# Issuing the first half of the first K load ahead of the wq load in a decode-attention kernel

## Chip, cores and metric

The kernel runs on one core of one Trainium2 chip. The metric is device time in microseconds (us) of one execution; lower is better. Five engines work side by side: TensorE (PE) for matmuls and transposes, VectorE (DVE) and ScalarE (ACT) for element-wise work, GpSimd (POOL), and SyncE (SP), which here only issues transfers. They are carried by 16 DMA engines.

A ratio is formed by the measuring program from the fast runs of both kernels in the same rounds; it is not quite the ratio of the medians quoted beside it, and its 95% interval is 3 to 4 us wide. The experiments ran in three sets of rounds, each on another chip, and each is compared with the kernel before in its own rounds.

## The reference

One token attends over a cache of 65,536 positions in 8 K/V heads of 256 elements, with 16 query heads; a small token-mixer branch and a gate are added. Cut to what matters:

```python
q = (x @ wq).reshape(B, Sq, Hq, Dh).transpose(0, 2, 1, 3)      # x: 1 x 448, wq: 448 x 4096
scores = jnp.einsum("bhqd,bhkd->bhqk", q, k) * (Dh ** -0.5)    # k: 8 heads x 65536 x 256
p = _softmax(scores, axis=-1)
o = jnp.einsum("bhqk,bhkd->bhqd", p, v)                        # v as k
a = o.transpose(...).reshape(B, Sq, Hq * Dh) @ wo
# ... b: layernorm, gelu mixer on the same token; g: sigmoid gate
return g * a + (1 - g) * b
```

K and V are 268 MB each in bf16. Everything else is small: wq is 3.67 MB, wo as much.

## The kernel before

The cache is walked in 32 rounds, each with one K load and one V load of 8.39 MB (64 KB a partition). K goes into a ring of one and a half loads (`kring`), V into one buffer (`vbuf`). SyncE issues every large load, in this order of waits (ScalarE issues the few small ones):

```python
@block.sync
def _(eng):
    eng.dma_start(wq_a..., A_wq[0:WF * P, :]...).then_inc(sem_wq, 16)     # 3.15 MB, into vbuf
    eng.dma_start(wq_b, A_wq[WF * P:DM, :]...).then_inc(sem_wq, 16)       # 0.52 MB, into vbuf
    for j in range(NP):                                                   # NP = 32
        if j >= 1:
            eng.wait_ge(sem_tr[NB - 1], BODY * (j - 1) + DC)   # half of K(j-1) transposed
        if j == 0:
            load(kring, A_k_cache, j, HV, NV, 0, sem_k)        # first half of K0
            load(kring, A_k_cache, j, 0, HV, 0, sem_kb)        # second half of K0
        # ... last round in halves
        else:
            load(kring, A_k_cache, j, 0, NV, HV * (j % 2), sem_k)
        if j == 0:
            eng.wait_ge(s_q, 1)                                # the query is computed: wq is free
            eng.wait_ge(s_hb, 1)
        else:
            eng.wait_ge(sem_pv, j)                             # V(j-1) is used up
        load(vbuf, A_v_cache, j, 0, NFIRST if last else NV, 0, sem_v)
        # ... at the first round of a head: the wo rows of that head
```

V0 overwrites the part of `vbuf` in which wq lies, so it waits for the query. V1 overwrites V0, so it waits until TensorE has done the whole first round: the query, 128 column groups of K0 transposed, scored and turned into weights, then 128 matmuls on V0:

```python
for g in heads:  for m in rounds_of_a_head:        # hardware loops
    keys(c0, j, u16, ...)      # transposes (line 298), scores (318)
    values(j, c0, u16)         # 128 matmuls on vbuf (358), the last one raises sem_pv
```

The softmax here doesn't subtract the row's maximum and nothing guards it: scores larger than these inputs give would overflow.

Of the kernel before, what the change touches and what calls it, by code (L numbers as in the profile page):

```python
# [12 lines left out]
def bass_gated_mix__gqa_block_cached__mixer_token_mlp__decode_kernel(  # L13
# [20 lines left out]
    DM = A_x.shape[-1]  # L34
# [4 lines left out]
    P = 128  # L39
# [17 lines left out]
    WF = 3  # L57
# [34 lines left out]
    with ctx:  # L92
# [6 lines left out]
        def new_sem(name):  # L99
            return ctx.enter_context(nc.semaphore(name))  # L100
# [22 lines left out]
        wq_a = early[:, 0:WF * NQ].rearrange("p (j n) -> p j n", j=WF)  # L123
        wq_b = early[:, WF * NQ:WF * NQ + HALF]
# [57 lines left out]
        sem_wq = new_sem("sem_wq")  # L182
# [36 lines left out]
        def src(cache, j, n0=0, n1=NV):  # L219
            g, m = divmod(j, PPH)  # L220
            s = cache[0, g, m * BODY * CH:(m + 1) * BODY * CH, :].rearrange("(p n) d -> p n d", p=P)
            return s[:, n0:n1, :].rearrange("p n d -> p (n d)")

        @block.sync
        def _(eng):
            eng.dma_start(wq_a.rearrange("p j n -> p (j n)"),  # L226
                          A_wq[0:WF * P, :].rearrange("(p j) n -> p (j n)", p=P)).then_inc(sem_wq, 16)
            eng.dma_start(wq_b, A_wq[WF * P:DM, :].rearrange("r (a n) -> (r a) n", a=2)  # L228
                          ).then_inc(sem_wq, 16)
            def load(dst, cache, j, n0, n1, at, sem):  # L230
                eng.dma_start(dst[:, at + n0:at + n1, :].rearrange("p n d -> p (n d)"), src(cache, j, n0, n1)  # L231
                              ).then_inc(sem, 16)

            for j in range(NP):
                last = j == NP - 1
                if j >= 1:
                    eng.wait_ge(sem_tr[NB - 1], BODY * (j - 1) + DC)
                if j == 0:
                    load(kring, A_k_cache, j, HV, NV, 0, sem_k)
                    load(kring, A_k_cache, j, 0, HV, 0, sem_kb)  # L240
                elif last:
                    load(kring, A_k_cache, j, 0, HV, HV, sem_k)
                    load(kring, A_k_cache, j, HV, NV, HV, sem_kb)
# [3 lines that stand above are left out]
                    eng.wait_ge(s_q, 1)  # L247
                    eng.wait_ge(s_hb, 1)
                else:
                    eng.wait_ge(sem_pv, j)  # L250
                load(vbuf, A_v_cache, j, 0, NFIRST if last else NV, 0, sem_v)
                if last:
                    for (n0, n1), sem in zip(pieces, sem_vp):
                        load(vbuf, A_v_cache, j, n0, n1, 0, sem)
                g, m = divmod(j, PPH)
                if m == 0 and g < H - 1:
                    if g >= 1:
                        eng.wait_ge(s_proj, g)
                    w = A_wo[g * REP * DH:(g + 1) * REP * DH, :]
                    eng.dma_start(wo_rows, w.rearrange("(p i) n -> p (i n)", i=2 * REP)).then_inc(sem_wo, 16)  # L260

            eng.wait_ge(s_proj, H - 1)
            for h in range(REP):
                w = A_wo[(HQ - REP + h) * DH:(HQ - REP + h + 1) * DH, :]
                eng.dma_start(wo_sb[:, h, :], w.rearrange("(p j) n -> p (j n)", j=2)).then_inc(sem_wl[h], 16)  # L265
            eng.wait_ge(s_fin, NCG)
            eng.dma_start(out_ap, out_row[:, :]).then_inc(sem_out, 16)
            eng.wait_ge(sem_out, 16)
# [13 lines left out]
        def _(pe):  # L282
# [86 lines left out]
            def piece_wait(n):  # L369
                for (n0, _), sem in zip(pieces, sem_vp):  # L370
                    if n == n0:
                        pe.wait_ge(sem, 16)
# [335 lines left out]
```

## Time and profile before

| | before |
|---|---|
| median of 6 executions | 1265.95 us (1265.83 to 1266.22) |
| span of the profiled execution | 1264.0 us |
| SyncE's DMA queue under way | 99.7% of 16 engines' span |
| rate from HBM | 431 GB/s |
| TensorE busy | 73% |

The kernel is a stream of loads. Two numbers describe each load: when SyncE issues it, and when it lands (its issue plus the "us to landing" of the DMA view). If each load is issued well ahead of the landing of the one in front of it, the queue never stands. This is the **lead**.

### The profile page before, as it was taken

What the parts mean: (1) busy time and instruction counts of PE and PEld (TensorE: products, weight loads), DVE (VectorE), ACT (ScalarE), POOL (GpSimd) and SP (SyncE); (2) the same over time, 40 slices, a digit from 0 to 9 for tenths busy, and PEclk for the clock granted to TensorE, in tenths of its full rate; (3) what the DMA queues carried; (4) which work ended last, traced back from release to release, by engine and by line L of the source; (5) the groups of instructions that cost most, each with busy time, mean ns of one, the idle gap of its engine ahead of it and who ended that gap; (6) DMA issues with size and microseconds to landing.
All of it is one profiled execution on the core that took longest, in us unless ns stands there. A gap on an engine that the chain in (4) does not pass through costs nothing.

```text
span 1264.0 us, 38850 instructions
## 1 busy us (share of the span) xinstructions
PE 917.0 (73%) x17114; PEld 868.4 (69%) x17114; DVE 422.5 (33%) x764; ACT 538.2 (43%) x788; POOL 0.9 (0%) x7
## 2 busy tenths in 40 slices
PE   3876678766778667786676876758767688676688
PEld 2766668766677666786666876658766578666687
DVE  2433344333444333443222332323322233332233
ACT  1443345533355433454333553335533355433455
POOL 0000000000000000000000000000000000000000
PEclk9887788787898887987888987889887888877999
DMA  9999999999999999999999999999999999999998
GB/s 411 428 434 436 433 431 431 431 438 431 433 433 433 433 431 438 425 433 440 431 436 429 431 431 433 440 433 433 431 431 431 438 436 433 431 433 431 431 427 367
DMA packets 11623, 544.39 MB, mean 431 GB/s; under 512 B 1369, under 2 KB 1628, under 8 KB 2908
## 3 DMA queue, kind: packets, MB, share of 16 engines
q1 hardware_dynamic: 11522, 544.22, 99.7%
q8 instruction: 8, 0.13, 0.0%
q10 hardware_dynamic: 90, 0.01, 0.0%
q14 instruction: 3, 0.02, 0.0%
HBM read 544.22 MB, written 0.00 MB: 431 GB/s over the span
## 4 chain that ended last, share of the span: by engine, by line
DMA 70%; PE 29%; issue 1%; SPq 0%; DVEq 0%; DVE 0%; ACT 0%; ACTq 0%
DMA kring<-in_A_k_cache_dram 68%; PE kst L298 24%; PE sps L318 4%; DMA wo_sb<-in_A_wo_dram 2%; PE acc L358 0%; SPq L231 0%; SPq L265 0%; SPq L228 0%; SPq L226 0%; PE prj L405 0%; PE acc L347 0%; DVEq L92 0%; DVE out_row L634 0%; ACT pT L658 0%; ACTq L658 0%
## 5 line engine op out<-in xcount | busy, mean ns | idle before, releaser
L298 PE MATMUL kst<-ident,kring 128*128 128x128 f32 x4096 | 563.7, 299 | 304.9 <-DMA kring<-in_A_k_cache_dram 294.1
L669 ACT ACTIVATE ktT<-kst 128x1024 bf16<-128x1024 bf16 x512 | 500.0, 1021 | 667.3 <-PE kst L298 666.5
L298 PEld LDWEIGHTS kst<-ident,kring 128*128 128x128 f32 x4096 | 514.0, 156 | 314.8 <-issue 312.2
L569 DVE COPY ktT<-kst 128x1024 bf16<-128x1024 bf16 x512 | 354.2, 692 | 765.0 <-PE kst L298 742.0
L318 PEld LDWEIGHTS sps<-qcur,ktT 128*128 128x128 bf16 x8192 | 237.8, 96 | 4.1 <-issue 1.6
L318 PE MATMUL sps<-qcur,ktT 128*128 128x2 bf16 x8192 | 236.6, 163 | 1.3 <-issue 1.3
L358 PE MATMUL acc<-vbuf,pT 128*2 128x256 bf16 x4080 | 140.4, 305 | 3.8 <-issue 3.3
L358 PEld LDWEIGHTS acc<-vbuf,pT 128*2 128x2 bf16 x4080 | 105.2, 93 | 30.6 <-issue 3.8
L658 ACT ACTIVATE pT<-sps 128x32 f32 x256 | 51.8, 202 | 16.4 <-PE sps L318 16.4
L347 PE MATMUL acc<-pT,ones_sq 128*128 128x32 bf16 x256 | 11.7, 178 | 12.3 <-ACT pT L658 12.3
L347 PEld LDWEIGHTS acc<-pT,ones_sq 128*128 128x128 bf16 x256 | 8.6, 96 | 15.2 <-ACT pT L658 14.9
L675 ACT ACTIVATE z_b<-z_b 128x448 bf16<-128x448 bf16 x14 | 8.1, 577 | 20.5 <-DVE z_b L556 20.4
L575 DVE COPY accs<-acc 128x288 f32<-128x288 f32 x8 | 3.7, 458 | 38.5 <-PE acc L358 38.5
L394 PEld LDWEIGHTS acc<-sel,accs 128*64 128x64 f32 x112 | 10.8, 214 | 0.9
L394 PE MATMUL acc<-sel,accs 128*64 128x1 f32 x112 | 11.4, 260 | 0.0
L431 PE MATMUL acc<-vbuf 42*128 42x42 bf16 x1 | 0.2, 214 | 8.3 <-DMA b_b<-in_B_b_dram 8.3
L405 PE MATMUL prj<-wo_sb,oTn 128*1 128x112 bf16 x128 | 3.7, 244 | 3.1 <-DVE oTn L600 2.9
L431 PEld LDWEIGHTS acc<-vbuf 42*128 42x128 bf16 x1 | 0.1, 102 | 8.4 <-DMA b_b<-in_B_b_dram 8.4
L562 DVE TENSOR_TENSOR gu<-wtmp,z_b 128x448 bf16<-128x448 bf16 x14 | 5.5, 393 | 1.0
L554 DVE TENSOR_TENSOR z_b<-u_b,wtmp 128x448 bf16<-128x448 bf16 x14 | 5.5, 393 | 1.0
L550 DVE TENSOR_TENSOR z_b<-wtmp,u_b 128x448 bf16<-128x448 bf16 x14 | 5.5, 393 | 1.0
L548 DVE TENSOR_TENSOR wtmp<-u_b 128x448 bf16<-128x448 bf16 x14 | 5.5, 392 | 1.1
(89 smaller groups left out, 82.5 us busy)
## 6 DMA issues: line engine op xcount, KB each, us to landing
kring<-in_A_k_cache_dram SPq DMA_DIRECT2D x4, 4096.0 KB, 24.3
vbuf<-in_A_v_cache_dram SPq DMA_DIRECT2D x1, 6144.0 KB, 25.7
wo_sb<-in_A_wo_dram SPq DMA_DIRECT2D x7, 448.0 KB, 27.6
vbuf<-in_A_wq_dram SPq DMA_DIRECT2D x1, 3072.0 KB, 10.2
vbuf<-in_A_v_cache_dram SPq DMA_DIRECT2D x1, 1024.0 KB, 27.8
vbuf<-in_A_v_cache_dram SPq DMA_DIRECT2D x1, 768.0 KB, 28.9
vbuf<-in_A_wq_dram SPq DMA_DIRECT2D x1, 512.0 KB, 10.9
vbuf<-in_A_v_cache_dram SPq DMA_DIRECT2D x31, 29.7
```

The lines of the kernel that those rows point to most:

```text
L298: ins = pe.transpose(kst[:, b, i * P:(i + 1) * P], kring_f[:, at + NT * (k % DC) + 4 * b + i, :], ident[:, :])
L318: ins = pe.matmul(sps[:, par, 2 * nt:2 * nt + 2], ktT[:, par, b, ntl * DH + dj:(ntl + 1) * DH:2], qcur[:, dj, :], start=(dj == 0), stop=(d ...
L347: pe.matmul(acc[:, DENC:SELC], ones_sq[:, :], pT[:, r, :], start=False, stop=(r == BODY - 1), skip_group_check=True)
L358: ins = pe.matmul(acc[o:o + REP, 0:DH], pT[:, r, 2 * nt:2 * nt + 2], vbuf[:, n, :], start=False, stop=False, skip_group_check=True)
L394: ins = pe.matmul(dst[hh * HP:(hh + 1) * HP, i:i + 1], accs[:, i:DH:2 * REP], sel[:, hh:hh + 1], start=False, stop=True, skip_group_check= ...
L548: vec.tensor_tensor(W, U, U, op=ALU.mult)
L550: vec.tensor_tensor(Z, W, U, op=ALU.mult)
L554: vec.tensor_tensor(Z, U, W, op=ALU.add)
L569: vec.tensor_copy(ktT[:, k % KTB, b, :], kst_b[:, b, :]).then_inc(sem_ev[b], 1)
L658: act.activation(pT[:, bass.ds(p0 + k % DC, 1), :].rearrange("p o n -> p (o n)"), sps[:, k % 2, 0:2 * NT], AF.Exp, scale=scale).then_inc(s ...
L669: act.activation(ktT[:, k % KTB, b, :], kst_b[:, b, :], AF.Copy).then_inc(sem_ev[b], 1)
L675: act.activation(z_b[:, :], z_b[:, :], AF.Tanh).then_inc(s_tanh, 1)
```

## The change

Before, PE sits idle for 9.5 us between the end of the query work and the first K transposes. The change lets the first half of K0 come in before wq, so that K should be there when PE gets to it. Nothing is removed or added.

```diff
         def _(eng):
-            eng.dma_start(wq_a.rearrange("p j n -> p (j n)"),
-                          A_wq[0:WF * P, :].rearrange("(p j) n -> p (j n)", p=P)).then_inc(sem_wq, 16)
-            eng.dma_start(wq_b, A_wq[WF * P:DM, :].rearrange("r (a n) -> (r a) n", a=2)
-                          ).then_inc(sem_wq, 16)
 ...
                 if j == 0:
                     load(kring, A_k_cache, j, HV, NV, 0, sem_k)
+                    eng.dma_start(wq_a.rearrange("p j n -> p (j n)"),
+                                  A_wq[0:WF * P, :].rearrange("(p j) n -> p (j n)", p=P)).then_inc(sem_wq, 16)
+                    eng.dma_start(wq_b, A_wq[WF * P:DM, :].rearrange("r (a n) -> (r a) n", a=2)
+                                  ).then_inc(sem_wq, 16)
                     load(kring, A_k_cache, j, 0, HV, 0, sem_kb)
```

## The prediction

> **What bounds the kernel now.** I read the page first: who is busy, and the chain that ended last.
>
> ```profile
> span 1264.0 us, 38850 instructions
> ...
> PE 917.0 (73%) x17114; PEld 868.4 (69%) x17114; DVE 422.5 (33%) x764; ACT 538.2 (43%) x788; POOL 0.9 (0%) x7
> ...
> q1 hardware_dynamic: 11522, 544.22, 99.7%
> ...
> HBM read 544.22 MB, written 0.00 MB: 431 GB/s over the span
> ...
> DMA 70%; PE 29%; issue 1%; SPq 0%; DVEq 0%; DVE 0%; ACT 0%; ACTq 0%
> ```
>
> The queue that SyncE (SP) fills has packets under way for 99.7% of 16 engines' span, while TensorE (PE) has a quarter of the span free. The chain names DMA for 70% and PE for 29%, but a chain that goes from a load's landing back to its issue and from there to the PE work that freed the buffer does not say that the queue was empty while PE worked. So the second view is when each load is issued and when it lands. The lines below are the queue's own timeline for the first 110 us.
>
> ```profile
> 0.74 0.41 SPq L226 DMA_DIRECT2D vbuf<-in_A_wq_dram  x1
> 1.20 0.41 SPq L228 DMA_DIRECT2D vbuf<-in_A_wq_dram  x1
> 1.67 1.10 SPq L231 DMA_DIRECT2D kring<-in_A_k_cache_dram  x2
> 17.54 0.33 SPq L231 DMA_DIRECT2D vbuf<-in_A_v_cache_dram  x1
> 17.91 0.43 SPq L260 DMA_DIRECT2D wo_sb<-in_A_wo_dram  x1
> 38.79 0.33 SPq L231 DMA_DIRECT2D kring<-in_A_k_cache_dram  x1
> 63.58 0.33 SPq L231 DMA_DIRECT2D vbuf<-in_A_v_cache_dram  x1
> ```
>
> The DMA view, narrowed to the issue of one load at a time, gives the time from issue to landing: wq's large part 10.2 (lands at 10.9), its small part 10.9 (12.1), the first half of K0 21.4 (23.1), the second half of K0 30.6 (about 32.9, issued at about 2.35), V0 34.8 (52.3), K1 34.1 (72.9), V1 28.6 (92.2). The landings of whole 8 MiB loads lie 19.4 to 20.6 us apart (20.6 where the 0.46 MB of wo lie between), and 8.39 MB at 431 GB/s is 19.5 us: one load follows the other without a gap, and each is issued 4 to 15 us before the one ahead of it lands (V0 at 17.5 against 32.9, K1 at 38.8 against 52.3, V1 at 63.6 against 72.9). This is a stream bound by bytes from the first microsecond to the last; the compute after the last landing is some 3 us.
>
> The third view is PE at the start, from the timeline:
>
> ```profile
> 16.09 0.55 PE L447 MATMUL prj<-vbuf,ones_sq 1*128 1x448 bf16 x1
> ...
> 17.50 0.36 PE L399 MATMUL prj<-zrow,ones_sq 1*128 1x224 bf16 x1 [0.59 <-DVE hbT L609]
> ...
> 27.41 6.17 PE L298 MATMUL kst<-ident,kring 128*128 128x128 f32 x32 [9.54 <-issue]
> ```
>
> PE ends the query work at 17.9 and starts the first K transposes at 27.4. Of that gap, 5.2 us pass until the first half of K0 lands (23.1), and in the chain of waits the other 4.34 us stand as "issue". This gap is what the change could be after.
>
> **What the Trainium skill says.** "DMA: Bandwidth & Descriptors", section "Where 436 GB/s comes from", gives a ceiling of 435 GB/s for the 16 DMA ports. The trace agrees: 431 GB/s over the span. The same page, "Queues, rings and completion order", says that each DMA engine consumes one queue's descriptors in ring order; the landings above come in the order of issue. So the change moves wq's landing back by the time of what is put ahead of it, and saves no byte. "Issuing engines are not separate DMA queues" says that ScalarE's (ACT's) small loads share the same 16 engines; in the trace the last of them lets PE go on only at 11.1, when wq is nearly in. "Runtime: NRT & Kernel Launch", section "Instruction fetch mechanics", says that a taken branch to code outside the loaded window makes the sequencer wait for a DMA fetch. The 4.34 us of "issue" at the entry of the loop would fit that, and the DMA view has a few packets of an instruction queue there; that they are one thing no view proves.
>
> **The change part by part.** Four issues stand in a new order: K0 first half, wq large, wq small, K0 second half. Nothing is removed or added; bytes (544.22 MB) and issue time (about 0.4 us each) stay.
>
> 1. First half of K0: 4.19 MB at 431 GB/s is 9.7 us. As first load it should land at about 12, since wq's 3.67 MB landed at 12.1 and the two are nearly of one size.
> 2. wq then lands behind 4.19 + 3.67 = 7.86 MB, the same bytes as the first half of K0 had up to its own end before: about 23.1 in place of 12.1. That is 11 us later.
> 3. The query chain follows. Before, its first matmul began at 12.58 and V0 was issued at 17.54, which is 4.96 us for 128 matmuls, the copies and the broadcast of h. Before, it was released by the small loads (11.05 to 12.37), now by wq: start at about 23.3, V0 issued at about 28.2 in place of 17.5. V0 cannot go earlier, since it overwrites the buffer in which wq lies.
> 4. Is the queue dry by then? Ahead of V0 lie the same 12.06 MB as before, which end at 32.9. First data moved at about 1.75 for an issue at 0.74, so 1.0 us of latency: 32.9 - 28.2 - 1.0 = 3.7 us to spare. Nothing is lost.
> 5. PE enters the K loop at about 28.5 with K0's first half long there. If the 4.3 us of code entry come after that point, transposes start at about 32.8, some 5.4 us later than before; if they were hidden, at 28.5. At worst everything in the first round shifts by 5.4 us: K1 issued at 44.2 (V0 ends at 52.3: 8.1 to spare), V1 at 69.0 (K1 ends at 72.9: 3.9 to spare, 2.9 after latency).
> 6. K1 lands at 72.9 as before, since the queue never ran dry, and PE, free at 66.1 + 5.4 = 71.5, waits for it. From there both kernels are the same.
>
> The sum: 0 us removed from the path, 0 to 0.3 us added by accident. I expect 1266.1 us.
>
> **The rivals.** First, the **intended gain**: K is there earlier, PE starts earlier, and the 9.5 us of idle PE come off the end, 1257 us. For it speaks only the gap itself. Against it: wq is on PE's path as well and moves back by as much as K moves forward, and PE time is not what the end waits for. I give it hardly any chance; and even that would be 0.8%, within the 2%. Second, a **dry queue**: the query chain is later by 11 us, and the slack of V0 falls from about 14 to 3.7 us, that of V1 from about 8 to 2.9. If the small loads, behind larger K packets (32 KB a partition in place of 24), came far later than now, or if code entry or a lower PE clock (0.50 to 0.75 between 54 and 70 us) stretched the first round by 4 to 5 us more, the queue would stand for 1 to 3 us and the end would move as much: 1267 to 1269 us. This is the likeliest miss. Third, a **better or worse start of the stream**: the rate was 393 to 396 GB/s from 3 to 7 us, while wq came in, against 431 later. If that is wq's shorter rows and not the start itself, moving them changes nothing (the same rows are still read); if wq beside K packets goes better or worse, it is worth at most 4 us x 9%, some 0.4 us either way.
>
> **Range and chances.** The three runs before span 0.4 us, and two loadings of one program may differ a little more, so I take 1.3 us downward; upward a little more for the dry queue: 1264.8 to 1267.8. A move over 2% would be 25 us, more than a whole 8 MiB load, and no term here comes near it: faster 0.01, same 0.98, slower 0.01.
>
> **What would show it right or wrong.** In the changed profile: the first half of K0 lands near 12, wq near 23; V0 is issued near 28 and lands again near 52; K1 lands near 73; the transposes begin between 28 and 33; the DMA rate over the span stays 431 GB/s. Wrong in step 2 if wq lands much before 20, in step 4 if V0 lands later than about 53, in step 5 if V1 is issued after 72 and lands after 93. I would be wrong altogether if a landing after 73 us differed from before by more than 2 us.

## The result and the profile after

The changed kernel took **1267.99 us** (median of 6 executions, 1267.51 to 1269.68) against 1265.95 us before; the ratio is 1.0017 with a 95% interval of 1.0005 to 1.003. It is slower by 2 us, which counts as the same at 2% but lies just above the predicted range (1264.8 to 1267.8).

The page of the changed kernel's profile answers to the one of before:

```profile
span 1265.8 us, 38850 instructions
...
PE 916.3 (72%) x17114; PEld 864.4 (68%) x17114; DVE 422.6 (33%) x764; ACT 537.8 (42%) x788; POOL 0.9 (0%) x7
...
q1 hardware_dynamic: 11522, 544.22, 99.6%
...
HBM read 544.22 MB, written 0.00 MB: 430 GB/s over the span
...
DMA 68%; PE 30%; issue 2%; SPq 0%; DVE 0%; ACT 0%; DVEq 0%; ACTq 0%
```

The same bytes, the same work, a span 1.8 us longer and a queue under way for 99.6% in place of 99.7%. An average over 1266 us can hardly show 2 us. The queue's timeline shows where to look. Its columns are start, duration, sequencer, line, operation, target and source, number of issues:

```profile
0.74 0.41 SPq L227 DMA_DIRECT2D kring<-in_A_k_cache_dram  x1
1.20 0.41 SPq L236 DMA_DIRECT2D vbuf<-in_A_wq_dram  x1
1.67 0.42 SPq L238 DMA_DIRECT2D vbuf<-in_A_wq_dram  x1
2.13 0.51 SPq L227 DMA_DIRECT2D kring<-in_A_k_cache_dram  x1
26.49 0.33 SPq L227 DMA_DIRECT2D vbuf<-in_A_v_cache_dram  x1
26.86 0.43 SPq L260 DMA_DIRECT2D wo_sb<-in_A_wo_dram  x1
46.38 0.33 SPq L227 DMA_DIRECT2D kring<-in_A_k_cache_dram  x1
70.47 0.33 SPq L227 DMA_DIRECT2D vbuf<-in_A_v_cache_dram  x1
```

V0, K1 and V1 are issued 8.9, 7.6 and 6.9 us later than before. For V1, the DMA view gives the issue-to-landing time, first of the kernel before, then of the changed one:

```profile
vbuf<-in_A_v_cache_dram SPq DMA_DIRECT2D x1, 28.6
```

```profile
vbuf<-in_A_v_cache_dram SPq DMA_DIRECT2D x1, 23.7
```

Put together, issue plus time to landing for each load of the two profiled executions:

| load | before: issued, landed | after: issued, landed |
|---|---|---|
| K0 first half | 1.7, 23.1 | 0.7, 13.0 |
| wq (small part, last) | 1.2, 12.1 | 1.7, 21.5 |
| K0 second half | 2.1, 32.8 | 2.1, 32.7 |
| V0 | 17.5, 52.3 | 26.5, 52.1 |
| K1 | 38.8, 72.9 | 46.4, 72.5 |
| V1 | 63.6, **92.2** | 70.5, **94.2** |
| K2 | 83.8, 111.6 | 84.2, 113.5 |
| wo, last load but one | 1231.6, 1260.8 | 1234.3, 1262.8 |

Up to K1 the changed stream is level or 0.4 us ahead. At V1 it is 2.0 us behind, and it stays so to the end: after V1 the loads land 19.35 us apart in both kernels. So the loss arises at one place, V1. It was issued 2.0 us before K1 had all landed, where before it was issued 9.3 us ahead. The rate over 5 us stretches says the same. The columns are the stretch and its length, the busy time (and number of instructions) of PE, of PE's weight loads, of DVE, ACT and POOL, then the granted share of PE's clock, the DMA share and GB/s. First before, then after:

```profile
65.00:70.00 5.00, 0.22 (x4) 0.09 (x4) 0.00 (x0) 0.00 (x0) 0.00 (x0) 0.66 1.03 446
70.00:75.00 5.00, 2.03 (x10) 2.03 (x11) 0.69 (x1) 0.00 (x0) 0.00 (x0) 0.50 0.99 423
```

```profile
65.00:70.00 5.00, 4.67 (x92) 3.06 (x96) 0.00 (x0) 0.00 (x0) 0.00 (x0) 0.51 0.97 419
70.00:75.00 5.00, 1.70 (x24) 1.27 (x17) 0.00 (x0) 0.00 (x0) 0.00 (x0) 0.83 0.99 370
```

From 70 to 75 us the changed kernel moves 370 GB/s, before 423. (A packet is counted where it starts, so single short stretches jump about.) PE is busy for 4.67 of 5 us with the last V0 matmuls from 65 to 70 us, work that was over before: V1 waits for it.

Why was PE so late? Below are the lines of PE at the start, after. The brackets hold PE's idle time before the line and what ended it; "issue" means that the profile shows nothing that PE waited for.

```profile
25.04 0.55 PE L447 MATMUL prj<-vbuf,ones_sq 1*128 1x448 bf16 x1
...
26.45 0.36 PE L399 MATMUL prj<-zrow,ones_sq 1*128 1x224 bf16 x1 [0.59 <-DVE hbT L609]
...
35.85 5.33 PE L298 MATMUL kst<-ident,kring 128*128 128x128 f32 x32 [9.03 <-issue]
```

K0's first half had landed at 13.0, and still PE stood for 9.03 us from the end of its query work to the first transpose. Before, with K0's half landing in the middle of the gap, it stood for 9.54 us. The gap that the change was to close was therefore not a wait for K. In that gap the DMA view shows two blocks of an instruction queue in both kernels. The columns are packets, MB and share. First before, 17.5 to 27.5 us, then after, 26.5 to 36 us:

```profile
q8 instruction: 2, 0.03, 1.3%
```

```profile
q8 instruction: 2, 0.03, 1.4%
```

In the trace these two blocks of 16 KB start at 18.7 and 24.6 us before, and at 27.0 and 33.1 us after. PE starts 2.8 us after the start of the second one in both. The other ten profiles agree: the gap runs from 6.9 to 11.5 us, but PE always starts 2.7 to 2.9 us after the start of the second block. This fits code being fetched for the first pass of the loop, behind the data on the same DMA engines; no run changed the code to test it.

### The profile page after: what moved, and what is told of

It is laid out like the page before. It is cut to its first block, busy times and chain, and to the rows that moved or that the text cites. A ratio compares the mean times of both kernels' runs of the same rounds, so it can differ in the third digit from the quotient of the medians.

```text
span 1265.8 us, 38850 instructions
## 1 busy us (share of the span) xinstructions
PE 916.3 (72%) x17114; PEld 864.4 (68%) x17114; DVE 422.6 (33%) x764; ACT 537.8 (42%) x788; POOL 0.9 (0%) x7
## 3 DMA queue, kind: packets, MB, share of 16 engines
q1 hardware_dynamic: 11522, 544.22, 99.6%
## 4 chain that ended last, share of the span: by engine, by line
DMA 68%; PE 30%; issue 2%; SPq 0%; DVE 0%; ACT 0%; DVEq 0%; ACTq 0%
DMA kring<-in_A_k_cache_dram 64%; PE kst L298 24%; PE sps L318 5%; DMA wo_sb<-in_A_wo_dram 2%; DMA vbuf<-in_A_wq_dram 2%; PE acc L358 1%; PE sps L441 0%; SPq L227 0%; PE sps L443 0%; PE acc L347 0%; DVE hbT L609 0%; PE prj L447 0%; SPq L265 0%; SPq L236 0%; ACT pT L658 0%
## 5 line engine op out<-in xcount | busy, mean ns | idle before, releaser
L298 PE MATMUL kst<-ident,kring 128*128 128x128 f32 x4096 | 557.5, 297 | 298.2 <-DMA kring<-in_A_k_cache_dram 287.1
L298 PEld LDWEIGHTS kst<-ident,kring 128*128 128x128 f32 x4096 | 507.7, 154 | 308.1 <-issue 305.5
L358 PE MATMUL acc<-vbuf,pT 128*2 128x256 bf16 x4080 | 146.0, 312 | 3.9 <-issue 3.4
L441 PE MATMUL sps<-xcol,vbuf 128*128 128x1 bf16 x96 | 3.5, 165 | 5.7 <-DMA vbuf<-in_A_wq_dram 5.7
L441 PEld LDWEIGHTS sps<-xcol,vbuf 128*128 128x128 bf16 x96 | 3.5, 104 | 5.8 <-issue 5.8
(89 smaller groups left out, 84.2 us busy)
## 6 DMA issues: line engine op xcount, KB each, us to landing
vbuf<-in_A_v_cache_dram SPq DMA_DIRECT2D x1, 768.0 KB, 28.2
```

What stands on the lines that cost most here:

```text
L298: ins = pe.transpose(kst[:, b, i * P:(i + 1) * P], kring_f[:, at + NT * (k % DC) + 4 * b + i, :], ident[:, :])
L358: ins = pe.matmul(acc[o:o + REP, 0:DH], pT[:, r, 2 * nt:2 * nt + 2], vbuf[:, n, :], start=False, stop=False, skip_group_check=True)
L441: pe.matmul(sps[:, 1, j:j + 1], wq_a[:, kt, col + dj:col + DH:2], xcol[:, kt:kt + 1], start=(kt == 0), stop=False)
```

## The experiments

The theory, called A in the expectations: the 2 us are a queue that runs dry at V1, because wq behind K delays the query, the query delays PE's first round, and V1 waits for that round. The rivals: B, the order of loads costs by itself; C, the lateness of PE is handed on to the end by itself.

### V1 issued late in the kernel before

This makes the lead zero without touching the order or PE.

```diff
                 else:
                     eng.wait_ge(sem_pv, j)
+                    if j == 1:
+                        eng.wait_ge(sem_k, 32)
```

> The kernel before, with one wait more on SyncE: V1 (the second V load) is issued only once K1 has landed (near 73 in place of 63.6). Order of the first four loads and all TensorE work stay. Theory A (the 2 us of the change are a dry queue at V1, which was issued 2.0 us ahead of K1's end): here the lead is 0, so V1 lands near 95.5 to 97 in place of 92.2 and the run takes 1269.5 to 1270.5 us. Rival B (K ahead of wq makes the start of the stream slower): that order is not here, so 1266.0. Rival C (the lateness of TensorE in the first round is handed on to the end): TensorE is not late before V1, so 1266.0 as long as the queue does not matter.

Measured: 1269.44 us (1268.62 to 1269.60, 5 executions) against 1265.96; ratio 1.0028, interval 1.0014 to 1.0041. The queue's timeline:

```profile
39.59 0.33 SPq L231 DMA_DIRECT2D kring<-in_A_k_cache_dram  x1
72.85 0.33 SPq L231 DMA_DIRECT2D vbuf<-in_A_v_cache_dram  x1
```

K1 landed at 72.8 and V1 at 94.65, sooner than the 95.5 expected at the least, and nothing made it up later; the median lies just under the expected range. A late V1 alone, with the old order and PE on time, costs more than the change does. Rivals B and C expected 1266.0: neither is needed for a loss of this size. Whether they add to the loss of the change, this run can't say; the next ones can.

### A smaller part of K ahead of wq

The 64 columns of the first half are cut at 32 (half) or 48 (three quarters), the rest follows wq. The waits of PE are counted accordingly.

```diff
-                    load(kring, A_k_cache, j, HV, NV, 0, sem_k)
+                    load(kring, A_k_cache, j, HV, HV + 32, 0, sem_kb)      # or HV + 48
                     ... wq_a, wq_b ...
+                    load(kring, A_k_cache, j, HV + 32, NV, 0, sem_k)
                     load(kring, A_k_cache, j, 0, HV, 0, sem_kb)
 ...
                 if k == 0:
                     pe.wait_ge(sem_k, u16)
+                    pe.wait_ge(sem_kb, 16)
                 if k == DC:
-                    pe.wait_ge(sem_kb, 16)
+                    pe.wait_ge(sem_kb, 32)
                     with pe.If(j == NP - 1):
-                        pe.wait_ge(sem_kb, 32)
+                        pe.wait_ge(sem_kb, 48)
```

> The changed kernel with only half of the first half of K0 (2.1 MB, 4.9 us) ahead of wq and the other half behind it. Theory A: wq lands near 16.6, V0 is issued near 21.7, V1 near 66.5 with some 5.5 to 6 us of lead over K1's end at 72.6; no dry queue, V1 lands near 92.1, time 1266.0 as before. Rival B: the harm goes with the bytes of K ahead of wq, so about half of it stays: 1267.0. Rival C: TensorE is late by half as much: 1267.0.

Measured for half: 1265.67 us (1265.56 to 1265.93) against 1265.96; ratio 0.9998, interval 0.9984 to 1.0012. The interval alone would allow a loss of 1.5 us, but the slowest of the five runs, 1265.93, lies below the median of the kernel before, whose own runs spread from 1265.83 to 1266.60. V1 was issued at 66.1 with K1 landing at 72.4, a lead of 6.3 us, and landed at 91.8:

```profile
66.14 0.33 SPq L227 DMA_DIRECT2D vbuf<-in_A_v_cache_dram  x1
```

Half of the bytes ahead of wq, and none of the harm. B and C expected half of it.

> The changed kernel with three quarters of the first half of K0 (3.1 MB, 7.3 us) ahead of wq. Theory A: V1 is issued near 68.3, lead about 4 us: the loss begins about here, 0 to 1.0 us, so 1266.0 to 1267.0. Rivals B and C: three quarters of the harm, 1267.5.

Measured for three quarters: 1265.86, 1266.56, 1268.12, 1268.28 and 1268.35 us, a median of 1268.12 against 1265.96 (ratio 1.001, interval 0.9996 to 1.0024). The expected range of 0 to 1 us was wrong: the loss is none, part or 2.4 us from one execution to the next. In the profiled one (1268.12) V1 had a lead of 3.7 us (68.83 against 72.58) and landed at 94.3:

```profile
68.83 0.33 SPq L227 DMA_DIRECT2D vbuf<-in_A_v_cache_dram  x1
```

In the trace each load counts 16 semaphore increments, read here as one from each DMA engine. Of V1's, 15 came by 92.6 us and the last at 94.3 (the next expectation gives both 0.3 us too late). The lag of 1.8 us stayed in every later load: the last increment of V30 came at 1223.5, the one before it at 1221.7.

The packets of the trace, which no view prints one by one, show where that engine lost its time. Its first V1 packet began at 73.03 us, 0.9 us after the last engine had ended K1. Later a 16 KB block of the instruction queue came between two of its packets (77.95 to 78.88), and the packet after it took 2.9 us in place of 2.4. So 1.4 of the 2.4 us came with that block, and not from the start of V1. In the kernel before, such a block came at 70.49 us, on one of the engines that ended K1 first, and cost nothing at the landing.

The same kernel was run again in other rounds:

> The kernel with three quarters of the half ahead again: its five times lay at 1265.9, 1266.6 and three times near 1268.2, in the fast state, and its profile was one of the late ones, where 15 of the 16 increments of V1's semaphore came by 92.9 and the last at 94.6. Theory A with a lead at the edge (V1 issued 3.8 us ahead of K1's last landing, the engines ending K1 over 2 us): each execution either catches one engine or does not, so both values again. If it is steady at one value, the spread has another cause.

Measured: 1266.76, 1267.10, 1267.71 and 1267.89 us. Spread, but not the same two values; each execution falls differently. In the profiled one V1 was issued at 70.8 with K1 landing at 72.7, a lead of 1.9 us, and landed at 93.7. PE stood 11.45 us at the entry of its loop, 2.4 us longer than in the first profile, so the lead varies too. Again the engine that ended V1 last had an instruction block between its packets (at 77.36). Whether it is this block that separates the fast executions of this kernel from the slow ones was not tested.

### All of K0 ahead of wq

```diff
                     load(kring, A_k_cache, j, HV, NV, 0, sem_k)
+                    load(kring, A_k_cache, j, 0, HV, 0, sem_kb)
                     ... wq_a, wq_b ...
-                    load(kring, A_k_cache, j, 0, HV, 0, sem_kb)
```

> The changed kernel with both halves of K0 (8.4 MB) ahead of wq. Theory A: wq lands near 31.5 to 32.5, the query chain of 5 us follows, V0 is issued near 37 with the queue dry since 32.5, so V0 lands near 59 to 60 in place of 52.1 (some 7 us lost), and K1 or V1 may lose 1 to 4 us more since their issue moves back too: 1274 to 1279. Rival B: twice the bytes ahead, twice the harm: 1270. Rival C: TensorE is later by another 10 us, all handed on: 1276 or more, but then with V0's landing unchanged near 52.

Measured: 1276.48 us (1274.45 to 1277.13); ratio 1.0081, interval 1.0067 to 1.0095. Now nothing is left to load while the query is computed, and the windows show it:

```profile
26.00:31.00 5.00, 0.00 (x0) 0.00 (x0) 0.00 (x0) 0.00 (x0) 0.00 (x0) 1.00 0.81 341
31.00:36.00 5.00, 4.31 (x131) 3.77 (x131) 0.95 (x4) 0.00 (x0) 0.00 (x0) 1.00 0.02 3
36.00:41.00 5.00, 0.36 (x1) 0.10 (x1) 0.10 (x1) 0.00 (x0) 0.00 (x0) 1.00 1.03 396
```

From 31 to 36 us the rate is 3 GB/s while PE does the 128 query matmuls. V0 lands at 59.9 (7.6 us late) and V1, with a lead of 2.5 us, at 101.4 (9.2 us late). V0's moved landing is what A expected and C did not.

### A cure: V loads cut in two

V1's first half needs only the first 64 columns of V0 to be used up, so it can be issued sooner. The first attempt cut every V load.

```diff
                 else:
+                    eng.wait_ge(sem_pvh, j)
+                load(vbuf, A_v_cache, j, 0, HV, 0, sem_v)
+                if j >= 1:
                     eng.wait_ge(sem_pv, j)
-                load(vbuf, A_v_cache, j, 0, NFIRST if last else NV, 0, sem_v)
+                load(vbuf, A_v_cache, j, HV, NFIRST if last else NV, 0, sem_v2)
 ...
-                some(0, NFIRST)
+                some(0, HV, sem_v).then_inc(sem_pvh, 1)
+                some(HV, NFIRST, sem_v2)
```

> The changed kernel with every V load cut in two halves: the first half is issued once TensorE has used the first 64 of the 128 value columns, the second half when all are used. K0's first half stays ahead of wq and the query chain stays late. Theory A (dry queue at V1): the first half of V1 is issued near 67 in place of 70.5, some 5 us ahead of K1's end at 72.5, the second half has a lead of over 10 us; the loss goes: 1265.7 to 1266.6. Any rival by which the order of the first loads, or the late first round of TensorE, costs time by itself: 1268.0 as the changed kernel.

> The same cut of the V loads in the kernel before, as control for the cut itself (twice the issues, 32 KB a partition in place of 64): no queue was dry there, so 1266.0, within 0.5 us, and the same as the changed kernel with the cut.

Measured: 1268.23 us (1268.03 to 1269.11) on the changed kernel and 1268.55 us (1268.19 to 1268.87) on the kernel before, both with a ratio of 1.0018 to the kernel before (1266.19 in these rounds). The expectation failed, and the control says why: the cut costs over 2 us by itself. The two orders no longer differ, and on the changed kernel V1 was all in at 92.0. The place was cured: K2 landed 0.25 us sooner than in the kernel before, where the change was 1.9 us late. But the cut costs some 0.08 us in each round of the run, in both orders, and this hides it. So the test was made again with V1 alone cut:

```diff
+                elif j == 1:
+                    eng.wait_ge(sem_pvh, 1)
+                    load(vbuf, A_v_cache, j, 0, HV, 0, sem_v)
+                    eng.wait_ge(sem_pv, 1)
+                    load(vbuf, A_v_cache, j, HV, NV, 0, sem_v1b)
                 else:
                     eng.wait_ge(sem_pv, j)
 ...
-                some(0, NFIRST)
+                some(0, HV).then_inc(sem_pvh, 1)
+                with pe.If(j == 1):
+                    pe.wait_ge(sem_v1b, 16)
+                some(HV, NFIRST)
```

> The changed kernel with V1 alone cut in two, the first half issued once TensorE has used 64 of V0's 128 value columns; every other load is whole. The cut of all V loads cost 2 us by itself in both orders, spread over the run, though V1 then landed at 92.0 as in the kernel before; with one load cut that cost should be 1/31 of it. Theory A: the first half is issued near 67.8, 4.5 to 5 us ahead of K1's last landing, V1 is all in near 92.1 and the time is 1265.8 to 1266.6. Rival (order of loads or TensorE's late first round cost time by themselves): 1267.5 to 1268.5 as the changed kernel.

> The same in the kernel before, as control: no dry queue to cure, so 1266.0 within 0.4 us. If this comes out at 1268, the test with one cut is as spoilt as the one with all.

Measured on the changed kernel: 1265.98 us, from 1265.65, 1265.68, 1265.98, 1266.87 and 1267.80; on the kernel before 1266.31 us (1266.00 to 1266.42); the kernel before itself 1266.05. Both ratios are 1.0002, interval 0.9988 to 1.0016. With V1 able to start sooner, three of five executions of the changed order are as fast as the old one (1265.62 to 1266.31 in these rounds); the other two are 0.8 and 1.8 us over its median. The interval alone hardly excludes the loss of the change (1.0016 is 2.0 us), and the uncut changed kernel was not run in these rounds, so this test supports A less firmly than the ones above. The profiled execution was the 1266.87 us one. PE entered its loop late there (11.2 us in place of 9.0), and the first of the two issues below had a lead of only 2.4 us over K1's landing at 72.4; V1 was all in 1.2 us late:

```profile
69.98 3.37 SPq L229 DMA_DIRECT2D vbuf<-in_A_v_cache_dram  x2
```

The changed kernel itself was measured again, in the rounds of the cut of all loads:

> The changed kernel again, in the same rounds as the two with the cut: 1267.5 to 1268.5, V1 issued near 70.5 and landed near 94.2. If it came out at 1266 here, the whole effect would be one of the day and nothing is left to explain.

Measured: 1265.85, 1266.93, 1268.39, 1269.33 and 1269.79 us, a median of 1268.39 against 1266.19 (ratio 1.0012, interval 0.9999 to 1.0026). One execution in five lost nothing and two lost over 3 us; this spread is itself a finding, since the kernel before keeps within 0.8 us in every set of rounds. The profiled one (1269.33) had V1 issued later than expected, 0.6 us after K1 had landed, and V1 landed at 95.1:

```profile
73.14 0.33 SPq L227 DMA_DIRECT2D vbuf<-in_A_v_cache_dram  x1
```

PE had entered its loop as in the first profile (transposes at 35.8 us), but began the V0 matmuls at 63.5 in place of 60.9. The fifth and sixth blocks of the instruction queue came as much later (58.3 and 65.4 in place of 55.8 and 62.8). This fits a spread that comes from code being fetched; it was not tested.

All profiled executions in which V1 is one load follow. V1's delay is its landing less K1's, less the 19.35 us that this takes in the kernel before. The last column takes the delay apart on the engine that ended V1 last, from its packets: how long after the last engine had ended K1 its first V1 packet began, what this packet took over the steady 2.42 us, and what an instruction block cost.

| run | lead of V1, us | delay at V1, us | late start + slow first packet + block |
|---|---|---|---|
| before | 9.3 | 0 | none |
| half ahead | 6.3 | 0.0 | none |
| three quarters ahead | 3.7 | 2.4 | 0.9 + 0.1 + 1.4 |
| all ahead | 2.5 | 1.8 | 1.1 + 0.7 + 0 |
| the change | 2.0 | 2.3 | 1.3 + 1.1 + 0 |
| three quarters, again | 1.9 | 1.7 | 0.3 + 0.0 + 1.4 |
| V1 late in the kernel before | -0.1 | 2.5 | 1.7 + 1.0 + 0 |
| the change, again | -0.6 | 3.2 | 2.7 + 0.6 + 0 |

A lead of 6.3 us or more cost nothing. At 3.7 us and less, 1.7 to 3.2 us were lost, not in strict order of the lead, and in two of the six 1.4 us of it fell to the instruction block. The parts add up to the delay within 0.2 us. One load with a lead between the two was on time: in the profile of the cut V1, K1 was issued 4.2 us before the wo load in front of it had landed, and landed 19.36 us after that load. Rivals B and C are left without support: the changed order is 0.35 us ahead when K1 lands, and with half ahead TensorE is late too (V1 was issued 2.6 us later than before) and nothing is lost. No version was clearly faster than the kernel before; half ahead is level with it.

## Why the prediction was wrong

**The bound and the absence of a gain were right.** The kernel is bound by its loads; PE's idle time at the start costs nothing, so K there sooner gains nothing. The first rival, a gain of 9.5 us, was rightly set aside.

**Steps 1 to 4 held**, with K0's first half landing at 13.0 rather than 12, wq at 21.5 rather than 23.1, and V0 issued at 26.5 rather than 28.2. V0 landed at 52.1, so its lead of 6 us was enough. One reading was loose: the loads are said to be issued 4 to 15 us ahead of the landing in front, but the three pairs given there are 9 to 15 us apart.

**Step 5 failed, in two of its terms.** It took the 9.5 us gap apart as a wait for K (to 23.1) and 4.3 us of code entry after it. The runs showed that the entry takes about 9 us, sometimes 11, by itself: 9.03 us with K there since 13.0, and 8.9 and 9.05 us with half and three quarters of the half ahead. The wait for K lay inside it. So the transposes began at 35.85 us where the prediction allowed 32.8 at the latest. V1 was issued at 70.5 where it allowed 69.0; the difference is smaller because the first round, from the first transpose to the last V0 matmul, took 34.6 us in place of 36.1. The profile of before had held a warning: the row said "9.54 <-issue", not a DMA. The chain of waits had put the first part of it down to the load, which landed in between; but with the load there long before, the gap was nearly as long.

The second term is what a lead is worth. The prediction subtracted 1.0 us of latency from the lead of 3.9 us and took the rest as spare. This 1.0 us is the time from the first issue of the kernel to the first packet of all. The packets of the traces give the time from V1's issue to its first packet on each of the 16 engines: 1.0 to 1.7 us with the queue empty (V1 late), and 1.0 to 2.9 us in the change. With three quarters ahead it was 4.2 us on an engine that had stood free for at least 0.9 us of it. Also, the engines do not end K1 together (last packets from 70.1 to 72.1 us in the changed kernel), so the early ones stood idle until V1's packets began at 71.4. And all 16 first packets of V1 took 2.6 to 3.5 us, against 2.42 for a packet in the steady stream. On the engine that ended last, the first packet began at 73.35, 1.3 us after the last engine had ended K1, and took 1.1 us too long: these are the 2.4 us. What the prediction had as 1.0 us was thus 2.9 on the engine that counts, with 1.1 more for a slow first packet. Why one engine gets its first packet so late, and why first packets are slow, stays open.

**Step 6 failed with it**, but for K1, which landed at 72.5 where 72.9 was forecast. K2 and all later loads are 2 us late: the loads land 19.35 us apart in both kernels, so nothing is made up, and the slowest DMA engine sets each landing.

**The second rival, a dry queue, is what happened**, with its predicted size (1267 to 1269 us); the prediction named it the likeliest miss. The kind of fault was foreseen, the size in part by luck: the rival asked for a first round longer by 4 to 5 us, and V1 was only 1.5 us later than step 5 allowed. By the prediction's own sum a lead of 2.0 us less 1.0 of latency would have cost nothing. The range should have reached beyond 1269. The third rival, the order at the start, is worth at most the 0.4 us by which K1 landed sooner.

## What to carry to other kernels

In a stream bound by loads, moving one load ahead of another moves everything that hangs on the second one; follow it through every buffer that must come free, and compare each issue with the landing of the load in front of it. Count a lead of several microseconds as needed, not one: here the last of the 16 DMA engines began V1 2.9 us after its issue in the change and 4.2 us with three quarters ahead, free for a while though it was, and an engine that fell behind kept its lag to the end. Code that is fetched on the same DMA engines can take 1.4 us more from one of them. Idle time put down to "issue" should not be read as a wait for data just because data lands in it: ask what the gap would be if the data were there.

## What the Trainium skill lacked or had wrong

- How far ahead a load has to be issued so that the stream behind it does not stall is on no page that I read. Here a lead of 6.3 us or more cost nothing, and leads of 3.7 us and less went with 1.7 to 3.2 us lost.
- "DMA: Bandwidth & Descriptors", "Rules for kernel authors", gives at least 1 MiB a load for maximum bandwidth. At 4 MiB in place of 8 MiB for each V load the kernel before still went from 1266.19 to 1268.55 us, some 0.08 us a round. The page's table of sizes has rows for 1 MB and 16 MB and none between, and it has no figure for one size against another in a stream.
- "Runtime: NRT & Kernel Launch", "Instruction fetch mechanics", gives no size for the stall of a branch to code that is not loaded. Here PE stood 8.9 to 11.5 us at the entry of its loop, and 6.9 us where the queue was empty just before it, and in all 12 profiles it started 2.7 to 2.9 us after the start of the second of two 16 KB blocks on the instruction queue. That the blocks are the cause is read from their times, not tested.
